# An RWKV-5 block followed by top-1 experts: rows stored in thirds, unpadded loads, weights and gathers asked for at other moments

## The chip, the cores and the metric

The kernel runs on one core of a Trainium2 chip. The core has a matrix engine (TensorE, PE in the profile, with PEld for its weight loads), VectorE (DVE), ScalarE (ACT), GpSimd (POOL), and SyncE (SP), which here does nothing but issue transfers. Sixteen DMA engines move data between device memory (HBM) and on-chip memory (SBUF); each engine's program issues its transfers in program order and waits on semaphores in that order too. The metric is the device time of one execution in microseconds (us), the median of several runs.

## The reference, cut to what matters

First comes an RWKV-5 recurrence over 4 batches, 8 heads, 768 steps and head size 48. Its result, 3072 rows of 384 numbers, goes through a switch layer: each row is sent to one of 8 experts (384 to 1024 to 384) by the largest gate logit, and scaled by its softmax weight.

```python
# attention: r, k, v (4, 8, 768, 48), w, u (8, 48)
state = np.zeros((B, H, D, D))
for t in range(S):
    kt, vt, rt = k[:, :, t], v[:, :, t], r[:, :, t]
    cur = np.einsum('bhd,bhe->bhde', u[None] * kt, vt)
    y[:, :, t] = np.einsum('bhd,bhde->bhe', rt, state + cur)
    state = w[None, :, :, None] * state + np.einsum('bhd,bhe->bhde', kt, vt)
x = y.transpose(0, 2, 1, 3).reshape(3072, 384)
# experts: w_gate (384, 8), w1 (8, 384, 1024), w2 (8, 1024, 384)
logits = x @ w_gate
expert_idx = np.argmax(logits, axis=1)
probs = softmax(logits)            # written out in the original
gate_w = probs[np.arange(N), expert_idx]
for e in range(E):
    mask = expert_idx == e
    out[mask] = gate_w[mask, None] * (np.maximum(x[mask] @ w1[e], 0.0) @ w2[e])
```

## The kernel before

The attention is worked off in 32 *units*: batch, half of the sequence (three chunks of 128 steps) and pair of heads, so that eight units make a batch and four a half. One turn of the loop over `u` loads unit u + 4, scales unit u + 2, forms the products of unit u + 1 and puts out unit u. Beside that, a half that is done goes through the gate (`u_gate`), and the rows of a done batch, with their gate weight as a 385th number, are stored to `x_hbm`, from where the expert part gathers them by index. The expert weights `w2` of all experts have one large tile; while the attention runs, the part for experts 4 to 7 serves as its ring of buffers.

```python
NW = E // 2                                    # 4 experts' w2 are loaded in the attention
ring = w2_all[:, NW:, :]                       # (flattened) the rest of w2's tile
rks = cut(4, 2 * HC * C)                       # r and k of a unit, 128 x 768 floats, 4 buffers
toks = cut(5, 4 * HC * D)                      # v and k by token, 128 x 576 floats, 5 buffers
...
xb_ring = cut(1, G * W)[0]...                  # rows of one batch, 6 x 385 floats per partition

def u_load(u):
    b, hf, hp = unit(u)
    nc.sync.dma_start(rks[u % 4], rk[b, hf, hp])      # heads at partitions 0-47 and 64-111, zeros between
    nc.sync.dma_start(toks[u % 5], tok[b, hf, hp])

def store_rows(b, xb, g0, g1):
    nc.sync.dma_start(x_hbm[b * S:(b + 1) * S, :]...[:, g0:g1], xb[:, g0:g1])

def weight():                                  # a step of choose(b, xb, lg)
    ...
    nc.vector.reciprocal(xb[:, :, DM], se)
    store_rows(b, xb, 0, HC)                   # first half of the batch's rows
return [shift, first, weight, lambda: store_rows(b, xb, HC, G)]
```

Scaling (lines 472 to 481) is what first needs a unit's loads:

```python
def u_scale(u, eng=nc.gpsimd):
    nc.gpsimd.tensor_tensor(x["RK"], x["r"], x["k"], op=ALU.mult)               # 472
    eng.tensor_tensor(x["K"], x["k"], bc(W2[:, hp, None, :], ...), op=ALU.mult) # 473
    nc.vector.tensor_tensor(x["R"], x["r"], bc(W1[:, hp, None, :], ...), op=ALU.mult)  # 474
def u_scale_g(u):
    nc.gpsimd.tensor_tensor(x["Kg"][:, 0:ns, :], x["kt"][:, 0:ns, :], ...)      # 481
```

The loop over units. `todo` holds the steps of the routing by turn: for batch b, with g = 8 (b + 1) + 2, `shift` in turn g, `first`, `weight` and the first store in g + 1, the second store in g + 2.

```python
for u in range(NU):
    if u + 4 < NU:
        u_load(u + 4)
    if HP <= u < HP + 4 * NW:
        w2_load((u - HP) // 4, u % 4, 4)       # a quarter of one expert's w2, 384 KB
    elif HP + 4 * NW <= u < HP + 4 * NW + NEARLY * FQ:
        tiles[(u - HP - 4 * NW) // FQ].load_w1(wp, u % FQ)
    if u + 2 < NU:
        u_scale(u + 2)
        u_scale_g(u + 2)
    if u + 1 < NU:
        if u:
            u_scores(u + 1)                    # products: lines 493, 503
        u_state(u + 1)
        u_mask(u + 1)
    u_out(u)
    ...
    for step in todo[u]:
        step()
```

Then comes the step to the experts. A *tile* is 128 rows of one expert: `load_x` gathers its rows (GpSimd, indirect), `turn` transposes them, `hidden` is the first product with ReLU (line 981), `result` the second (line 990) with the scaling by the gate weight, `store` scatters the rows to the output. Tiles t0 and t1 are known from the first two batches; their rows and w1 are loaded in the attention. All others need the last batch's routing (`ranks`, `bases`, `order`, `slots`, `owners`, `index`).

```python
weight()
rest()                                         # stores of the last batch's rows
w2_load(NW)
w2_load(NW + 1)                                # 1536 KB each
...
t2.load_w1(wp)
t0.result(mo)
t1.hidden(mo, 0)
R.index(rt, "rw")
t2.load_x(mo)
t3.load_x(mo)
t0.store()
for e in range(NW + 2, E):
    w2_load(e)
t1.hidden(mo, 1)
t3.load_w1(wp)
t1.result(mo)
t1.store()
t2.turn(mo, "g")
late = late_rows(R, NSURE - NEARLY, ...)       # 8 gathers: rows of tiles that run only if there are many
run_tiles(tiles[2:], wp, mo, Segments(R, 0))

def run_tiles(tiles, wp, mo, seg):
    for j, t in enumerate(tiles):
        if j + 2 < len(tiles):
            tiles[j + 2].load_x(mo)
        ...
        t.hidden(mo, 0)
        ...
        t.hidden(mo, 1)
        ...
        if j + 2 < len(tiles):
            tiles[j + 2].load_w1(wp)
        ...
        if j + 1 < len(tiles):
            tiles[j + 1].turn(mo, "g")
        t.result(mo)
        t.store()
```

`late_rows` makes up to 8 tiles whose rows are gathered in any case and which are computed only behind a test of a count; with these inputs none of them runs. Line numbers in the texts below are those of this kernel where it is the one spoken of.

Of the kernel before, what the change touches and what calls it, by code (L numbers as in the profile page):

```python
# [1 line left out]

# [20 lines left out]
HP = H // 2  # L23
# [18 lines left out]
NW = E // 2  # L42
# [9 lines left out]
def rwkv5_then_switch(ctx, tc, r, k, v, rk, tok, wu_in, wl, wg, wgh, w1, w2, out):  # L52
# [35 lines left out]
    xb_ring = cut(1, G * W)[0].rearrange("p (g d) -> p g d", g=G)  # L88

# [4 lines left out]
    def u_load(u):  # L94
        b, hf, hp = unit(u)
        nc.sync.dma_start(rks[u % 4], rk[b, hf, hp])
        nc.sync.dma_start(toks[u % 5], tok[b, hf, hp])
# [75 lines left out]
    def choose(b, xb, lg):  # L173
# [27 lines left out]
        return [shift, first, weight, lambda: store_rows(b, xb, HC, G)]  # L201

    def general():
# [166 lines left out]
        def gate(b, xb):  # L370
# [13 lines left out]
            for step in choose(b, xb, lg):  # L384
                step()

# [13 lines left out]
    def fast():  # L400
# [35 lines left out]
        def tables(hp):  # L436
            scaled(W2, Wr, hp, w_64)
            scaled(W1, Wp, hp, w_64)
# [131 lines left out]
        xbs = [xb_ring, la.tile([128, G, W], FP32, name="xb")]  # L570
# [50 lines left out]
        with tc.manual_schedule():  # L621
            tables(0)
# [52 lines left out]
            shift, first, weight, rest = chosen[B - 1]  # L675
# [4 lines left out]
            rest()  # L680
            w2_load(NW)
            w2_load(NW + 1)
# [243 lines left out]
    class Tile:  # L926
# [58 lines left out]
        def result(self, mo):  # L985
            p = self.R.ps.tile([128, DM], FP32, name="yp", tag="y", bufs=2)
            e = slice(self.j, self.j + 1) if self.early else ds(self.expert(ENG.PE), 1)
            for f in range(FT):
                rhs = w2_all[:, e, f * DM:(f + 1) * DM]
                nc.tensor.matmul(p, lhsT=self.hT[:, f, :], rhs=rhs, start=f == 0, stop=f == FT - 1)  # L990
# [73 lines left out]
    def run_tiles(tiles, wp, mo, seg):  # L1064


        for j, t in enumerate(tiles):
# [30 lines left out]
    def late_rows(R, first, rows):  # L1098


        late = [Tile(R, j, late=True) for j in range(first, NTILE)]
        late += [Segments(R, j, late=True) for j in range(1, E // NS)]
        for t, xs in zip(late, rows, strict=True):
            t.load_x(xs)
        return late
# [25 lines left out]
    def after_general():  # L1131
# [15 lines left out]
        with tc.manual_schedule():  # L1147
# [5 lines left out]
            late = late_rows(R, NSURE, [xl[:, i] for i in range(NTILE - NSURE + E // NS - 1)])  # L1153
            run_tiles(tiles, mo, mo, Segments(R, 0))
# [70 lines left out]
```

## Time and profile before

| | |
|---|---|
| device time, median of 3 runs | 442.06 us (441.38 to 442.60) |
| span of the profiled execution | 440.0 us |
| TensorE busy | 415.4 us (94%) |
| VectorE, ScalarE, GpSimd busy | 149.5, 127.5, 155.6 us |
| mean granted TensorE clock | 0.973 |
| moved by DMA | 101.7 MB, mean 231 GB/s |

The profile is one execution on the chip. A busy time is the sum of an engine's instructions. *The chain of waits* follows the execution back from its last instruction: at each step to what released it, or to the instruction before it on its engine; printed in order of time, its columns are the start, the duration, and what it was. *The timeline* lists instructions with start, duration, engine, line, operation, tiles and count; brackets hold the idle time in front and what ended it. SPq and POOLq are the issuing queues of SyncE and GpSimd: the duration there is that of the issue, not of the transfer. *The windows* give busy time of each engine in a stretch of time, the granted clock of TensorE, the share of time that the DMA engines were busy, and GB/s. The attention ends near 139 us (the first transposes of t0 stand at 139.07 us), t1's result at 164.7 us, the last matmul at 429.4 us.

### The profile page before, as it was taken

The numbers are of one execution on the slowest core, as the hardware profiler recorded it, in microseconds if no ns is written. First come the engines' busy times: TensorE is split into PE (matmuls) and PEld (weight loads), VectorE is DVE, ScalarE is ACT, GpSimd is POOL, SyncE is SP. The second block draws the span as 40 slices with busy tenths as digits, with TensorE's granted clock in tenths as the row PEclk, the third lists the DMA queues.
The fourth block names the chain that finished last, engine by engine and source line by source line (L and its number), as shares of the span: only waits on it lengthen the run. The fifth ranks groups of instructions, "written<-read, shape, count | busy, mean of one in ns | idle before, by whom it ended". The sixth has DMA issues, their size and how long they took to land.

```text
span 440.0 us, 10264 instructions
## 1 busy us (share of the span) xinstructions
PE 415.4 (94%) x4079; PEld 343.6 (78%) x4079; DVE 149.5 (34%) x407; ACT 127.5 (29%) x394; POOL 155.6 (35%) x189
## 2 busy tenths in 40 slices
PE   8899998997999997979999999999999999999990
PEld 8799997997999877758887878777878778787770
DVE  6576796896897840101111111010111111010100
ACT  3777775774765220101111111111110101111110
POOL 7997746945962027302111111111111101111100
PEclk9999999999899996989999999999999999999997
DMA  7488959959942899885886656665858585554100
GB/s 267 149 250 283 302 161 344 387 166 340 384 151 70 259 361 387 167 350 188 329 317 183 257 201 242 216 267 189 302 181 313 184 305 180 178 181 148 63 21 25
DMA packets 28704, 101.73 MB, mean 231 GB/s; under 512 B 4134, under 2 KB 7228, under 8 KB 25316
## 3 DMA queue, kind: packets, MB, share of 16 engines
q1 hardware_dynamic: 24642, 89.69, 57.2%
q0 software_dynamic: 3712, 11.23, 8.9%
q8 instruction: 37, 0.61, 0.6%
q14 instruction: 23, 0.19, 0.1%
q10 hardware_dynamic: 290, 0.02, 0.0%
HBM read 91.47 MB, written 9.65 MB: 230 GB/s over the span
## 4 chain that ended last, share of the span: by engine, by line
PE 81%; DMA 7%; POOL 3%; issue 3%; DVE 2%; ACT 1%; POOLq 0%; SPq 0%
PE hp L981 27%; PE yp L990 26%; PE P L503 5%; PE yp L564 4%; DMA w_all<-in_r_k_units_dram 4%; PE P L493 4%; DMA xs<-x_hbm,idx 3%; PE yp L560 3%; PE rp L593 3%; PE Gp L539 2%; PE xTp L968 2%; PE warm L110 2%; PE hg L1036 1%; PE yg L1056 1%; POOL xb L962 1%
## 5 line engine op out<-in xcount | busy, mean ns | idle before, releaser
L981 PEld LDWEIGHTS hp<-xT,w1s 128*128 128x128 f32 x1152 | 135.7, 195 | 11.2 <-issue 4.1
L981 PE MATMUL hp<-xT,w1s 128*128 128x128 f32 x1152 | 138.0, 279 | 0.6 <-DVE xT L970 0.6
L990 PE MATMUL yp<-w_all,hT 128*128 (+1 forms) x384 | 129.6, 491 | 0.6 <-ACT hT L983 0.6
L990 PEld LDWEIGHTS yp<-w_all,hT 128*128 128x128 f32 x384 | 71.8, 192 | 46.3 <-ACT hT L983 1.2
L983 ACT ACTIVATE hT<-hp 128x512 f32<-128x512 f32 x48 | 28.7, 597 | 238.0 <-PE hp L981 216.3
L995 POOL DMA_INDIRECT out_dram<-yo,idx x22 | 22.4, 1019 | 204.0 <-DVE yo L992 194.5
L514 ACT ACTIVATE A<-ident,dv 128x128 f32<-128x128 f32 x192 | 59.6, 389 | 0.2 <-ACT dv L511 0.2
L992 DVE TENSOR_SCALAR yo<-yp,xs 128x384 f32<-128x384 f32 x22 | 13.6, 618 | 106.2 <-PE yp L990 106.2
L970 DVE COPY xT<-xTp 128x384 f32<-128x384 f32 x23 | 12.8, 556 | 104.6 <-PE xTp L968 93.3
L472 POOL TENSOR_TENSOR w_all<-w_all 128x384 f32<-128x384 f32 x31 | 34.3, 1108 | 26.9 <-DMA w_all<-in_r_k_units_dram 13.0
L564 PE MATMUL yp<-A,w_all 128*64 128x128 f32 x384 | 41.5, 283 | 0.1
L525 DVE COPY_PREDICATED A<-mask,P 128x384 f32<-128x384 int32 x64 | 33.8, 583 | 8.0 <-ACT A L514 7.4
L560 PE MATMUL yp<-w_all,St 128*64 128x128 f32 x320 | 34.5, 282 | 0.2 <-ACT dv L511 0.2
L473 POOL TENSOR_TENSOR w_all<-w_all,W 128x384 f32<-128x384 f32 x31 | 33.6, 1085 | 0.0
L962 POOL DMA_INDIRECT xs<-x_hbm,idx x22 | 21.5, 976 | 31.6 <-PE hp L981 25.5
L503 PE MATMUL P<-w_all 48*128 48x128 f32 x384 | 30.2, 291 | 0.4
L493 PE MATMUL P<-wu,w_all 48*128 48x1 f32 x384 | 26.5, 249 | 4.0 <-POOL w_all L472 4.0
L493 PEld LDWEIGHTS P<-wu,w_all 48*128 48x128 f32 x384 | 24.0, 187 | 8.0 <-POOL w_all L472 4.5
L564 PEld LDWEIGHTS yp<-A,w_all 128*64 128x64 f32 x384 | 28.3, 142 | 0.9 <-DVE A L525 0.5
L474 DVE TENSOR_TENSOR w_all<-w_all,W 128x384 f32<-128x384 f32 x32 | 25.6, 804 | 6.9 <-DMA w_all<-in_r_k_units_dram 5.6
L481 POOL TENSOR_TENSOR w_all<-w_all,Wg 128x288 f32<-128x288 f32 (+1 forms) x32 | 24.9, 779 | 1.4 <-ACT dv L511 1.1
L503 PEld LDWEIGHTS P<-w_all 48*128 48x128 f32 x384 | 24.7, 191 | 0.8 <-POOL w_all L473 0.4
(164 smaller groups left out, 299.5 us busy)
## 6 DMA issues: line engine op xcount, KB each, us to landing
w1s<-in_moe_w_dram SPq DMA_DIRECT2D x22, 1536.0 KB
w_all<-in_r_k_units_dram SPq DMA_DIRECT2D x32, 384.0 KB
wq<-in_moe_w_dram SPq DMA_DIRECT2D x32, 384.0 KB
w_all<-in_v_k_units_dram SPq DMA_DIRECT2D x32, 288.0 KB
w_all<-in_moe_w_dram SPq DMA_DIRECT2D x16, 384.0 KB
w_all<-in_moe_w_dram SPq DMA_DIRECT2D x4, 1536.0 KB
w1s<-in_moe_w_dram SPq DMA_DIRECT2D x8, 384.0 KB
x_hbm<-w_all SPq DMA_DIRECT2D x4, 577.5 KB
```

Source lines behind the costliest of these rows:

```text
L472: nc.gpsimd.tensor_tensor(x["RK"], x["r"], x["k"], op=ALU.mult)
L473: eng.tensor_tensor(x["K"], x["k"], bc(W2[:, hp, None, :], [128, HC, C]), op=ALU.mult)
L493: nc.tensor.matmul(P[hi][:, o:o + 1], lhsT=x["RK"][q, c, :], rhs=wu[q, 1, hp:hp + 1], start=True, stop=True, skip_group_check=True)
L503: nc.tensor.matmul(P[hi][:, c * C:(c + 1) * C], lhsT=x["K"][q, c, :], rhs=x["R"][q, c, :], start=True, stop=True, skip_group_check=True)
L514: nc.scalar.activation(A[:, hi, c, :], ident, func=ACT.Copy, scale=dv[:, hi, c:c + 1])
L525: nc.vector.copy_predicated(A[:, hi], bc(mask[:, None, :].bitcast(I32), [128, HC, C]), P[hi][:, 0:HC * C].rearrange("p (c t) -> p c t", t=C))
L560: nc.tensor.matmul(yp[q, c, :], lhsT=old[:, hi, :], rhs=x["R"][:, c, :], start=True, stop=False, skip_group_check=True)
L564: nc.tensor.matmul(yp[q, c, :], lhsT=vh(x, c, hi, 64), rhs=x["A"][:, hi, c, :], start=old is None, stop=True, skip_group_check=True)
L962: nc.gpsimd.indirect_dma_start(out=self.xs, out_offset=None, in_=x_hbm[:, :], in_offset=off)
L981: nc.tensor.matmul(p[:, f, :], lhsT=self.w1[:, q, d, o:o + 128], rhs=self.xT[:, d, :], start=d == 0, stop=d == DT - 1)
L983: nc.scalar.activation(self.hT[:, 4 * fb:4 * fb + 4, :], p, func=ACT.Relu)
L990: nc.tensor.matmul(p, lhsT=self.hT[:, f, :], rhs=rhs, start=f == 0, stop=f == FT - 1)
```

## The change

Six things change. The rows of a batch go to memory in three parts of two chunks, one per turn in turns g + 1 to g + 3, and these turns carry no expert weights. Units from the fifth on load only the 48 rows of r and k that each head has, in two transfers; the padding stays zero from the first four. The rows of one batch move out of the ring, which then fits into three experts' place, so five experts' w2 are loaded in the attention instead of four, their pieces spread over the turns that store nothing, six of them ahead of the loop. The last three experts' w2 are asked for right behind the last batch's rows, where it was two there and two later. The transposes of t2 stand before the last two products of t1's result. And the eight late gathers are issued one per tile, from the seventh tile of the main loop on, where they stood together ahead of it. The purpose is to keep transfers that the next work waits for from queueing behind others. What is computed does not change.

```diff
-NW = E // 2
+NW = 5
-    xb_ring = cut(1, G * W)[0].rearrange("p (g d) -> p g d", g=G)
     def u_load(u):
         b, hf, hp = unit(u)
-        nc.sync.dma_start(rks[u % 4], rk[b, hf, hp])
+        if u < 4:
+            nc.sync.dma_start(rks[u % 4], rk[b, hf, hp])
+        else:
+            for hi in range(2):
+                q = slice(64 * hi, 64 * hi + D)
+                nc.sync.dma_start(rks[u % 4][q], rk[b, hf, hp, q])
         nc.sync.dma_start(toks[u % 5], tok[b, hf, hp])
 ...
             nc.vector.reciprocal(xb[:, :, DM], se)
-            store_rows(b, xb, 0, HC)
 ...
-        return [shift, first, weight, lambda: store_rows(b, xb, HC, G)]
+        return [shift, first, weight, lambda i, n: store_rows(b, xb, i * G // n, (i + 1) * G // n)]
 ...
-        xbs = [xb_ring, la.tile([128, G, W], FP32, name="xb")]
+        xbs = [ca.tile([128, G, W], FP32, name="xb0"), la.tile([128, G, W], FP32, name="xb1")]
 ...
+        stores = set()
         for b in range(B - 1):
             g = 2 * HP * (b + 1) + 2
-            for i in range(4):
-                todo[g + min(i, 1) + i // 3].append(lambda b=b, i=i: chosen[b][i]())
+            for i in range(3):
+                todo[g + min(i, 1)].append(lambda b=b, i=i: chosen[b][i]())
+            for i in range(3):
+                todo[g + 1 + i].append(lambda b=b, i=i: chosen[b][3](i, 3))
+                stores.add(g + 1 + i)
 ...
+        pieces = [lambda e=e, i=i: w2_load(e, i, 4) for e in range(NW) for i in range(4)]
+        n = 4 * (NW - 1)
+        pieces[n:n] = [lambda j=j, i=i: tiles[j].load_w1(wp, i) for j in range(NEARLY) for i in range(FQ)]
+        turns = [u for u in range(1, NU) if u not in stores]
+        ahead = len(pieces) - len(turns)
+        piece = dict(zip(turns, pieces[ahead:], strict=True))
         with tc.manual_schedule():
+            for load in pieces[:ahead]:
+                load()
 ...
-                if HP <= u < HP + 4 * NW:
-                    w2_load((u - HP) // 4, u % 4, 4)
-                elif HP + 4 * NW <= u < HP + 4 * NW + NEARLY * FQ:
-                    tiles[(u - HP - 4 * NW) // FQ].load_w1(wp, u % FQ)
+                if u in piece:
+                    piece[u]()
 ...
-            rest()
-            w2_load(NW)
-            w2_load(NW + 1)
+            rows(0, 2)
+            rows(1, 2)
+            for e in range(NW, E):
+                w2_load(e)
 ...
-            for e in range(NW + 2, E):
-                w2_load(e)
             t1.hidden(mo, 1)
             t3.load_w1(wp)
-            t1.result(mo)
+            t1.result(mo, lambda: t2.turn(mo, "g"))
             t1.store()
-            t2.turn(mo, "g")
-            late = late_rows(R, NSURE - NEARLY, [xbs[1][:, i] for i in range(G)] + [t0.xs, t1.xs])
-            run_tiles(tiles[2:], wp, mo, Segments(R, 0))
+            late = late_tiles_of(R, NSURE - NEARLY)
+            run_tiles(tiles[2:], wp, mo, Segments(R, 0), zip(late, [xbs[1][:, i] for i in range(G)] + [t0.xs, t1.xs],
+                                                             strict=True))
 ...
             for f in range(FT):
+                if within and f == FT - 2:
+                    within()
 ...
             t.result(mo)
             t.store()
+            if j >= 6:
+                for x, xs in islice(late, 1):
+                    x.load_x(xs)
```

(Cut: the same edits in the path for decays out of the usual range, which does not run with these inputs.)

More of the change, by code (lines that the diff above doesn't have):

```diff
@@ L1 @@
 from contextlib import ExitStack
+from itertools import islice
 import concourse.bass as bass
@@ L383, in gate @@
             nc.vector.tensor_copy(lg, lgp)
-            for step in choose(b, xb, lg):
+            *steps, rows = choose(b, xb, lg)
+            for step in steps:
                 step()
+            rows(0, 1)
         step = 0
@@ L674, in fast @@
             mo = em.enter_context(tc.tile_pool(name="mo", bufs=2))
-            shift, first, weight, rest = chosen[B - 1]
+            shift, first, weight, rows = chosen[B - 1]
             shift()
@@ L983, in hidden, with result @@
             nc.scalar.activation(self.hT[:, 4 * fb:4 * fb + 4, :], p, func=ACT.Relu)
-        def result(self, mo):
+        def result(self, mo, within=None):
             p = self.R.ps.tile([128, DM], FP32, name="yp", tag="y", bufs=2)
@@ L1062, in result, with run_tiles @@
             nc.vector.tensor_scalar_mul(self.y, self.p, self.xs[:, DM:W])
-    def run_tiles(tiles, wp, mo, seg):
+    def run_tiles(tiles, wp, mo, seg, late):
         for j, t in enumerate(tiles):
@@ L1096, in run_tiles, with late_tiles_of @@
                 seg.store()
[L1098 to L1105, printed above, removed]
+    def late_tiles_of(R, first):
+        return [Tile(R, j, late=True) for j in range(first, NTILE)] + \
+            [Segments(R, j, late=True) for j in range(1, E // NS)]
     def late_tiles(R, tiles):
@@ L1152, in after_general @@
             xl = rt.tile([128, NTILE - NSURE + E // NS - 1, W], FP32, name="xl")
-            late = late_rows(R, NSURE, [xl[:, i] for i in range(NTILE - NSURE + E // NS - 1)])
-            run_tiles(tiles, mo, mo, Segments(R, 0))
+            late = late_tiles_of(R, NSURE)
+            run_tiles(tiles, mo, mo, Segments(R, 0), zip(late, [xl[:, i] for i in range(len(late))], strict=True))
         em.close()
```

## The prediction

> **What bounds the kernel now.** I read the chain of waits first, because it says which engine's work sets the end.
>
> ```profile
> PE 81%; DMA 7%; POOL 3%; issue 3%; DVE 2%; ACT 1%; POOLq 0%; SPq 0%
> ```
>
> TensorE is the bound, and no part of the change removes a matmul. What can be won is TensorE's waiting, so I read the same chain in order of time and looked for long pieces that are not PE.
>
> ```profile
> 63.76 8.66 DMA w_all<-in_r_k_units_dram
> 72.58 0.57 POOL w_all L472
> ...
> 74.87 1.44 PE P L503 x12
> ...
> 97.24 9.06 DMA w_all<-in_r_k_units_dram
> ...
> 176.99 14.00 DMA xs<-x_hbm,idx
> 191.12 0.81 PE xTp L968 x3
> 191.93 6.60 PE yp L990 x16
> ```
>
> There are three: two loads of r and k that come late (units 17 and 25 of 32), and one gather of rows for the expert tiles. Third, busy time by stage. The columns after the stretch are its length, busy PE, PEld, DVE, ACT and POOL, granted clock, DMA share and GB/s.
>
> ```profile
> 72.00:76.00 4.00, 2.01 (x26) 1.88 (x24) 2.62 (x7) 0.77 (x3) 3.21 (x3) 0.89 1.03 405
> 76.00:80.00 4.00, 4.00 (x60) 3.65 (x59) 2.51 (x6) 2.83 (x10) 3.53 (x4) 0.68 1.04 400
> 164.00:168.00 4.00, 1.37 (x6) 0.39 (x4) 0.73 (x2) 0.00 (x0) 2.00 (x2) 0.91 1.05 414
> 168.00:172.00 4.00, 3.50 (x16) 3.50 (x17) 0.45 (x1) 0.00 (x0) 2.89 (x4) 0.50 0.96 390
> ```
>
> Each gap is paid twice: PE stands still, then runs at half clock for some microseconds. DMA is full in all four rows. Why the loads come late shows in SyncE's own timeline:
>
> ```profile
> 53.39 0.41 SPq L603 DMA_DIRECT2D w_all<-in_moe_w_dram  x1
> 60.71 0.39 SPq L171 DMA_DIRECT2D x_hbm<-w_all  x1
> ...
> 63.28 0.39 SPq L171 DMA_DIRECT2D x_hbm<-w_all  x1
> 63.76 0.44 SPq L96 DMA_DIRECT2D w_all<-in_r_k_units_dram  x1
> ```
>
> SyncE issues in order. It stands at the first store of a batch's rows for 6.9 us, until the gate weights exist, and then pours out two stores of 577.5 KB, with 672 KB of unit and 384 KB of expert weights for each turn between them. Last, the step from attention to the expert tiles:
>
> ```profile
> 159.33 5.33 PE L990 MATMUL yp<-w_all,hT 128*128 128x384 f32 x16
> 167.13 0.72 PE L968 MATMUL xTp<-ident,xs 128*128 128x128 f32 x3 [2.48 <-DMA xs<-x_hbm,idx]
> 168.50 8.30 PE L981 MATMUL hp<-xT,w1s 128*128 128x128 f32 x48 [0.65 <-DVE xT L970]
> 191.12 0.81 PE L968 MATMUL xTp<-ident,xs 128*128 128x128 f32 x3 [2.57 <-DMA xs<-x_hbm,idx]
> ```
>
> From 198.4 to 429.4 us PE is busy 4.00 of every 4 us; nothing is to be won there.
>
> [...] the load issued at 63.76 behind a store lands 8.66 us later. [...] issued from 159.49 to 160.48, the gather released PE at 167.1, so 6.6 us. I use 6.6. [...] Here gaps of 1.9 and 2.5 us were enough (0.50 from 168 to 173 us). [...] the multiplication of line 474 takes 0.55 us in the median and up to 3.05.
>
> **The change, part by part.**
>
> *Attention turns.* The cost of the two late loads comes from the starts of each unit's products (line 503) in PE's timeline. Units 5 to 13 take 29.2 us, units 13 to 21 take 33.5, units 21 to 29 take 34.5. In the undisturbed eight, the step into a second half (unit 9) is 3.27 us and the step after it 3.76. The same two steps take 5.47 and 5.37 us at units 17 and 18, so 3.8 us too much, and 5.79 and 5.38 at units 25 and 26, so 4.1 us too much. Together 7.9 us. (What is left over in those eights is the ranking matmuls, about 0.5 us a batch, and they stay.)
>
> Is this removed? SyncE still stands for the same 6.9 us, since the first third also waits for the weights. But behind it each of three turns now carries a third of the rows (385 KB) and an unpadded unit (48 of 64 rows of r and k: 288 KB, with v 576 KB) and no expert weights. Before, 2.98 MB moved from 61 to 72 us. Two stores are 1.18 MB; the rest at the 400 GB/s of the next row takes 4.5 us, which leaves 6.5 us, or about 180 KB/us, for the stores. After: two thirds at that pace 4.3 us, unit 16 and r, k of unit 17 (864 KB) 2.2 us. So unit 17's r and k land at about 61 + 6.5 + 1.5 = 69 us, an estimate, instead of 72.4; they are wanted at about 70.5 (PE would start that unit near 72, and line 472 takes 1.0). One to two microseconds of margin: I count both stalls as gone. The fourteen calm turns lose nothing: 576 + 384 KB in 3.76 us is 255 KB/us. The six weight pieces sent at the start (2.36 MB, 6 us) fall where DMA stood at 34% and 13% (12 to 20 us). One issue more per turn is 0.4 us of SyncE's 3.8.
>
> What takes something back is VectorE. Around the second stall it is busy 19.6 of 24 us (104 to 128); with the turns 4 us shorter that is 19.6 of 20. [...] I take back 1 us. Attention: -6.9 us.
>
> *First expert tile (t2).* Before, SyncE asked for experts 4 and 5 behind the last rows, for t2's first weights at 157.6, then for experts 6 and 7. Now expert 4 comes earlier and 5, 6 and 7 go right behind the rows. Bytes from 145.4 on: 1.18 + 4.72 MB. Before, 4.3 MB were through at 157.6; the remaining 1.57 MB take 3.8 us at 415 GB/s, so to 161.4; then t2's 1.57 MB, to 165.2; with its share for two gathers and completion, about 167. The gather of t2's rows is issued at the same moment against the same full DMA, so it should again land near 167. Two arrivals near 167 while PE is free at 163 to 165: **the first stall stays**. The transposes now stand before the last two products of t1's result (4 of the 16 records of 0.323 us): PE waits from 163.4 instead of 164.7, then has 1.3 us of work that covers the copy of 0.65. With half clock on it, even or 0.5 us worse. I take +0.5.
>
> *Second expert tile (t3).* The gather of 176.99 came behind eight late gathers, 1.3 us of issue each; they move into later tiles, so it is issued at 166.9 behind t1's store alone, and DMA is empty of bulk near 170. A calm tile takes 10.85 us (332.87 to 343.72 in the chain). Here, from 183.03 to 198.37, it took 15.34. Gain 4.5 us.
>
> *Later tiles.* Eight more gathers and their issue, one per tile, on a GpSimd that is busy 2 of 11 us. Nothing.
>
> Sum: 442.1 - 6.9 + 0.5 - 4.5 = 431.2 us.
>
> **The rivals.** *A: the first gather is freed too.* If the 6.6 us came from the three large loads queued at 158 and not from a full DMA as such, rows and weights might be there by 164. t2 then also runs at full clock: it lost 3.8 us of waiting and 14.53 - 10.85 = 3.7 us behind it, so up to 7 us more, about 424. For it: fewer bytes are left at 160 us (3.1 MB with t3's weights, where it was 5). Against: 3 MB is still 7 us of full DMA. I give it 0.25. *B: VectorE becomes the bound of the attention turns.* Then 3 to 4 us of the 7.9 stay, about 434. For it: 98% of the shortened stretch. Against: before the stall it idled 2.7 us waiting for the same load, and TensorE does not need a unit's mask until about 3 us after it. 0.2. *C: t2's weights come clearly later than the rows*, since they stand behind three experts instead of two: each microsecond beyond 167 costs one, with up to 3, about 434. 0.2. *D: late gathers among the tiles* hold back a tile's rows or weights. From 181 to 188 DMA moved only about 100 GB/s while gathers ran, so they are slow company; but rows are asked for nearly two tiles (20 us) ahead. 0.05.
>
> **Range and chances.** The middle is 431.2, with 0.25 x 7 us from A and smaller costs from B and C against it, so 430.0. Low end: A whole, 423.5. High end: B or C beside the rest, 435. Faster by 2% needs 433.2 or less; that fails only if attention gives 4 us or less, or if t2 loses 3: faster 0.80, same 0.19, slower 0.01.
>
> **What would show it.** In the changed profile the chain should hold no r, k load of 8 us; the steps into units 17, 18, 25 and 26 should be below 4.2 us; t2's transposes should still wait for rows or weights near 159 us (167 less 7 to 8) with half clock behind; t3 should take 10.9 us from hidden to hidden. The prediction is wrong if those steps stay above 5 us (the stores' issue, not their size, is the cause), if VectorE closes the gaps in PE, or if new waits stand among the later tiles.

## The result, and the profile after

The changed kernel takes 429.27 us (median; 426.78 to 430.15) where the kernel before took 442.33 us on the same chip: a ratio of 0.969, with a 95% interval of 0.963 to 0.975. The profiled execution has a span of 428.4 us, with TensorE busy for 408.6 us (95%). These lines of its page show the chain of waits by engine, and two groups: busy time and mean duration, then the idle time just before them and what ended most of it.

```profile
PE 88%; DMA 4%; DVE 1%; POOL 1%; issue 1%; ACT 0%; SPq 0%; POOLq 0%; DVEq 0%; ACTq 0%
...
L509 PE MATMUL P<-w_all 48*128 48x128 f32 x384 | 29.6, 286 | 1.5 <-DVE w_all L480 1.3
...
L499 PE MATMUL P<-wu,w_all 48*128 48x1 f32 x384 | 26.9, 249 | 1.3 <-POOL w_all L478 0.9
```

Line 509 is what was line 503, line 499 was 493, line 478 was 472. The load of r and k, twice in the chain of before with some 9 us each, does not end any idle time of TensorE now: what is left in front of the products is 1.3 us of VectorE, one wait ahead of unit 0 (9.34 us), and 0.9 us of GpSimd, one wait ahead of unit 29:

```profile
119.24 0.83 PE L499 MATMUL P<-wu,w_all 48*128 48x1 f32 x12 [0.90 <-POOL w_all L478]
```

SyncE's timeline at the first batch shows the thirds, one per turn, and that SyncE still stands in front of the first of them.

```profile
54.14 0.37 SPq L102 DMA_DIRECT2D w_all<-in_v_k_units_dram  x1
61.14 0.40 SPq L176 DMA_DIRECT2D x_hbm<-xb  x1
...
63.18 0.40 SPq L176 DMA_DIRECT2D x_hbm<-xb  x1
63.67 1.22 SPq L101 DMA_DIRECT2D w_all<-in_r_k_units_dram  x2
```

The loads of 63.67 are those of unit 17. GpSimd's timeline shows when they are there (the bracket is the idle time and what ended it):

```profile
71.20 1.22 POOL L478 TENSOR_TENSOR w_all<-w_all 128x384 f32<-128x384 f32 x1 [1.04 <-DMA w_all<-in_r_k_units_dram]
```

So they are there by 71.2 us, 1.4 us earlier than the 72.58 of before, and it is enough: the multiplication ends at 72.42, and TensorE comes to unit 17 at 72.91 without a wait. The step to the experts in TensorE's timeline:

```profile
153.33 4.04 PE L1009 MATMUL yp<-w_all,hT 128*128 128x384 f32 x12
160.71 0.88 PE L985 MATMUL xTp<-ident,xs 128*128 128x128 f32 x3 [3.35 <-DMA xs<-x_hbm,idx]
161.38 2.77 PE L1009 MATMUL yp<-w_all,hT 128*128 128x384 f32 x4
163.94 6.70 PE L998 MATMUL hp<-xT,w1s 128*128 128x128 f32 x48
...
175.97 5.52 PE L998 MATMUL hp<-xT,w1s 128*128 128x128 f32 x48
```

The first expert wait is still there (3.35 us, rows of t2), with half clock behind it; the second, at 191 us before, is gone. The windows (length, busy PE, PEld, DVE, ACT, POOL, granted clock, DMA share, GB/s) show the stretch around the second attention stall of before, now with VectorE and DMA nearly full and TensorE busy at full clock, and at the first expert tile a full DMA up to about 163 us and the clock at half behind the wait:

```profile
98.00:118.00 20.00, 19.71 (x365) 18.15 (x361) 18.44 (x49) 14.83 (x55) 14.78 (x17) 1.00 1.05 279
156.00:160.00 4.00, 1.37 (x5) 0.48 (x3) 0.00 (x0) 0.00 (x0) 1.02 (x1) 0.95 1.00 421
160.00:164.00 4.00, 3.29 (x8) 2.11 (x9) 0.56 (x1) 0.00 (x0) 0.00 (x0) 0.50 0.88 360
164.00:168.00 4.00, 4.00 (x27) 4.00 (x26) 0.62 (x1) 0.00 (x0) 1.99 (x2) 0.70 0.18 62
```

Where the time came from, read from the starts of the same instructions in both traces (us):

| stretch of TensorE's timeline | before | after | change |
|---|---|---|---|
| start to unit 0's products | 8.61 | 9.34 | +0.73 |
| unit 0 to unit 31 (attention) | 125.36 | 118.64 | -6.72 |
| unit 31 to t1's result | 25.36 | 25.35 | 0 |
| t1's result to t3's first hidden | 23.70 | 22.64 | -1.06 |
| t3's to t4's first hidden | 15.34 | 10.84 | -4.50 |
| t4's first hidden to the end | 241.63 | 241.59 | 0 |
| sum = difference of the spans | | | -11.6 |

Every microsecond is placed, but the first row's 0.73 has no account. Seven more traces with the changed attention (below) give 117.43 to 118.73 us for the second row, so such a stretch scatters over 1.3 us from trace to trace.

### The profile page after: what moved, and what is told of

It is laid out like the page before. It is cut to its first block, busy times and chain, and to the rows that moved or that the text cites. A ratio compares the mean times of both kernels' runs of the same rounds, so it can differ in the third digit from the quotient of the medians.

```text
span 428.4 us, 10349 instructions
## 1 busy us (share of the span) xinstructions
PE 408.6 (95%) x4079; PEld 338.2 (79%) x4079; DVE 146.6 (34%) x407; ACT 127.6 (30%) x394; POOL 152.5 (36%) x189
## 4 chain that ended last, share of the span: by engine, by line
PE 88%; DMA 4%; DVE 1%; POOL 1%; issue 1%; ACT 0%; SPq 0%; POOLq 0%; DVEq 0%; ACTq 0%
PE hp L998 28%; PE yp L1009 27%; PE P L509 6%; PE P L499 6%; PE yp L570 5%; PE rp L599 4%; PE yp L566 4%; PE Gp L545 3%; DMA w_all<-in_moe_w_dram 3%; PE xTp L985 2%; DMA xs<-x_hbm,idx 2%; PE hg L1055 1%; PE yg L1075 1%; PE warm L456 1%; POOL w_all L478 0%
## 5 line engine op out<-in xcount | busy, mean ns | idle before, releaser
L998 PE MATMUL hp<-xT,w1s 128*128 128x128 f32 x1152 | 136.4, 277 | 0.0
L570 PE MATMUL yp<-A,w_all 128*64 128x128 f32 x384 | 39.2, 274 | 0.1
L566 PE MATMUL yp<-w_all,St 128*64 128x128 f32 x320 | 32.4, 274 | 0.0
L479 POOL TENSOR_TENSOR w_all<-w_all,W 128x384 f32<-128x384 f32 x31 | 32.0, 1033 | 0.0
L570 PEld LDWEIGHTS yp<-A,w_all 128*64 128x64 f32 x384 | 25.6, 137 | 0.8 <-DVE A L531 0.5
L487 POOL TENSOR_TENSOR w_all<-w_all,Wg 128x288 f32<-128x288 f32 (+1 forms) x32 | 24.0, 751 | 4.1 <-ACT dv L517 2.0
L480 DVE TENSOR_TENSOR w_all<-w_all,W 128x384 f32<-128x384 f32 x32 | 23.3, 732 | 1.4 <-DMA w_all<-in_r_k_units_dram 1.3
```

Of the source, the lines that this page charges most:

```text
L479: eng.tensor_tensor(x["K"], x["k"], bc(W2[:, hp, None, :], [128, HC, C]), op=ALU.mult)
L566: nc.tensor.matmul(yp[q, c, :], lhsT=old[:, hi, :], rhs=x["R"][:, c, :], start=True, stop=False, skip_group_check=True)
L570: nc.tensor.matmul(yp[q, c, :], lhsT=vh(x, c, hi, 64), rhs=x["A"][:, hi, c, :], start=old is None, stop=True, skip_group_check=True)
L998: nc.tensor.matmul(p[:, f, :], lhsT=self.w1[:, q, d, o:o + 128], rhs=self.xT[:, d, :], start=d == 0, stop=d == DT - 1)
```

## The experiments

Absolute times differ from chip to chip (in the four sets of runs the kernel before took 442.33, 438.84, 437.44 and 438.78 us), so kernels are compared by their ratio to before or, more sharply, by the stretches of their traces. The kernels with padded loads, weights in store turns, and late gathers together or spread shared one chip; halves, all three undone, t3's weights behind the gather and two experts later a second; the rest a third.

### One measure of the attention undone at a time

Padded loads again:

```diff
-        if u < 4:
-            nc.sync.dma_start(rks[u % 4], rk[b, hf, hp])
-        else:
-            for hi in range(2): ...            # 48 rows of each head, 144 KB each
+        nc.sync.dma_start(rks[u % 4], rk[b, hf, hp])
```

> The changed kernel, but units from the fifth on load all 128 rows of r and k again, padding included, in one transfer of 384 KB instead of two of 144 KB. My theory in the prediction (fewer bytes buy the margin behind the stores): the loads behind the stores land about 1 us later, so the steps into units 17 and 25 go from 3.27 us to 4 to 5, and the time rises by 1 to 3 us (430 to 432). The rival (from the profile after: from 20 to 60 us SyncE's queue keeps the DMA engines busy 94.7% of the time for 10.15 MB, where before it was 77.9% for 10.25 MB, so a transfer to 48 rows is the dearer one): the queue's share falls back to about 78%, the steps stay below 4 us, and the time is the same within 1 us (428 to 430).

Weight pieces in the turns that store:

```diff
-        turns = [u for u in range(1, NU) if u not in stores]
+        turns = list(range(HP, HP + len(pieces) - 6))
```

> The changed kernel, but the 22 weight pieces of the loop stand in turns 4 to 25, as before, so that six of the nine turns that store a third also carry a piece of 384 KB. If keeping the weights out of the store turns is what frees the loads: the steps into units 17 and 18 and into 25 and 26 grow by 1 to 4 us in each of the two groups, and the time rises by 2 to 7 us (431 to 436). If thirds instead of halves are enough: no step above 4.5 us and the same time within 1 us.

Rows in two halves:

```diff
-            for i in range(3):
-                todo[g + 1 + i].append(lambda b=b, i=i: chosen[b][3](i, 3))
-                stores.add(g + 1 + i)
+            for i in range(2):
+                todo[g + 1 + i].append(lambda b=b, i=i: chosen[b][3](i, 2))
+            for i in range(3):
+                stores.add(g + 1 + i)
```

> The changed kernel with the rows of a batch stored in two halves again (turns g + 1 and g + 2) instead of three thirds; the turn g + 3 keeps its freedom from weights, and all else stays. Theory: what freed the loads is fewer bytes queued in front of unit 17's and 25's r and k; a half in front of them instead of a third is 193 KB more per turn, about 0.5 to 1 us at 180 to 400 KB/us, inside the margin of 1 to 2 us: units 13 to 21 and 21 to 29 stay within 1 us of the changed kernel's 30.30 and 31.68 us. Rival: the thirds are what counts, since a store moves slowly (180 KB/us); then the steps at 17 and 18 go back above 5 us each and each group of eight takes 33 us or more, 3 to 5 us more in all.

And the three edits together:

> The changed kernel with all three attention measures undone together: padded loads of r and k (384 KB), weight pieces in the turns that store, rows in two halves. What stays is five experts' weights in the attention, six pieces ahead of the loop, and all of the expert part. Singly, padding cost 1.1 us from unit 0 to unit 31 and weights in the store turns 3.5 us. Theory: the measures are one, namely bytes queued ahead of the load that the next turn wants; undone together they bring back both stalls whole, 6 to 8 us more than the changed kernel's 118.64 us (about 125 to 126). Rival: one measure alone does it; then the sum is near the largest single one, 3.5 to 4 us more, about 122.

Measured (steps between the starts of consecutive units' products; the undisturbed pair is 3.27 and 3.76 us):

| kernel | steps into 17, 18 | into 25, 26 | unit 0 to 31 | ratio to before, interval |
|---|---|---|---|---|
| before | 5.47, 5.37 | 5.79, 5.38 | 125.36 | |
| changed | 3.27, 3.76 | 3.27, 3.77 | 118.64 | 0.969 (0.963 to 0.975) |
| changed, again | 3.27, 3.76 | 3.27, 3.77 | 118.17 | 0.976 (0.971 to 0.981) |
| padded loads | 3.89, 3.87 | 3.27, 3.81 | 119.78 | 0.977 (0.968 to 0.986) |
| weights in store turns | 4.14, 4.50 | 3.97, 4.17 | 122.22 | 0.981 (0.973 to 0.989) |
| halves | 3.27, 3.76 | 3.83, 3.90 | 120.11 | 0.983 (0.977 to 0.989) |
| all three | 4.63, 3.89 | 5.08, 5.50 | 122.46 | 0.992 (0.989 to 0.994) |

By the ratios alone the three single edits can't be told from the changed kernel, which is 0.969 on one chip and 0.976 on another; what follows rests on one trace of each. No single measure brings a stall of before back. With padded loads the step into unit 17 is 3.89 us and the one into 25 unchanged, so below 4 as the rival said, not the 4 to 5 of the theory, and the DMA share is as the rival had it (below); of the 1.1 us more from unit 0 to unit 31, 0.7 us are lost there (steps into 17 and 18). Beside it, TensorE waits 1.12 us for VectorE ahead of unit 27, and not the 0.90 us for GpSimd ahead of unit 29. Weights in the store turns cost 1.6 us at units 17 and 18 and 1.1 at 25 and 26, the low end of what was expected. That edit costs 3.6 us in all, but not all of it is the queue: 2.2 us is one wait at unit 31, where GpSimd had two early gathers of rows to issue right ahead of the multiplication that TensorE wanted; without it this edit is worth no more than the other two. TensorE's and GpSimd's timelines of that kernel:

```profile
130.31 0.83 PE L499 MATMUL P<-wu,w_all 48*128 48x1 f32 x12 [2.24 <-POOL w_all L478]
```

```profile
126.25 1.25 POOL L975 DMA_INDIRECT xsA<-x_hbm,idxA  x1 [0.30 <-POOL xsA L974]
...
128.22 1.00 POOL L975 DMA_INDIRECT xsA<-x_hbm,idxA  x1 [0.28 <-POOL xsA L974]
129.25 1.00 POOL L478 TENSOR_TENSOR w_all<-w_all 128x384 f32<-128x384 f32 x1
```

The halves cost nothing at units 17 and 18 and 0.7 us at 25 and 26. The kernel with two experts' weights later (below) has thirds and 3.98 and 3.88 us at units 25 and 26, so it is not shown that thirds are worth anything over halves. (Another 1.75 us at unit 20 of that kernel, 5.51 instead of 3.76, has an idle time of 1.41 us that the profile gives no cause for; a step of 4.50 us stands at the same place in one kernel with thirds. It stays open, and it is the larger part of this kernel's 1.5 us.) With all three undone, the second stall is back nearly whole, 10.58 us for the two steps against 11.17 before. The first is not. TensorE's timeline of the kernel with all three undone shows why the two differ:

```profile
73.58 0.83 PE L494 MATMUL P<-wu,w_all 48*128 48x1 f32 x12 [1.02 <-POOL w_all L473]
...
105.29 0.83 PE L494 MATMUL P<-wu,w_all 48*128 48x1 f32 x12 [1.47 <-POOL w_all L473]
```

A wait of 1.02 us was followed by full clock (groups of four products at 0.39 us, as undisturbed; step 3.89), one of 1.47 us by half clock (granted 0.50 from 109 to 111 us, groups of four at 0.60 to 0.64 us; step 5.50), and before, 1.86 us by half clock too (0.50 from 76 to 78 us; step 5.37). Both theory (6 to 8 us back) and rival (3.5 to 4) put a number on this: 3.8 us came back in this trace, the rival's number (the traced run, 431.56 us, is among the faster of its kernel, whose median is 433.72, so that 3.8 is at the low end). But the rival's reason does not hold, since no measure alone brings a stall back and the second stall is nearly whole; the number is about what one whole stall makes. The 2.9 us that did not come back are 2.3 us at the first stall and 0.6 at the second; what else in the change holds them was not separated.

The four kernels order the same way at unit 17 by both measures. GpSimd starts its multiplication at 71.14 us with padded loads, at 71.69 with weights in the turns, at 72.25 with all three undone, at 72.58 before; the step into unit 17 is 3.89, 4.14, 4.63, 5.47 us. (Unit 16 began between 69.40 and 69.92 us in these four. In the first trace of the changed kernel it began at 70.33, so that 71.20 was still in time; in its second at 69.57, with the multiplication at 70.22.)

Padded loads had a surprise: the unpadded ones are the dearer for DMA. The calm stretch from 20 to 60 us in the windows of the changed kernel, and then of the one with padded loads:

```profile
20.00:60.00 40.00, 40.00 (x746) 36.90 (x744) 28.21 (x76) 30.43 (x112) 31.13 (x41) 1.00 0.96 257
```

```profile
20.00:60.00 40.00, 40.00 (x743) 36.95 (x743) 30.48 (x75) 30.82 (x114) 34.12 (x43) 1.00 0.81 279
```

The last two numbers are the DMA share and GB/s: with unpadded loads the engines are busy 0.96 of the time for 257 GB/s, with padded ones 0.81 for 279 (before: 0.79 for 259). The issues of the same stretch (KB each, median us to landing), changed and then padded:

```profile
w_all<-in_r_k_units_dram SPq DMA_DIRECT2D x20, 144.0 KB, 7.4
```

```profile
w_all<-in_r_k_units_dram SPq DMA_DIRECT2D x9, 384.0 KB, 5.3
```

Fewer bytes, and they land 2 us later. Why is not shown: the unpadded load writes 48 partitions at a time where the padded one writes 128, and it is two transfers of 144 KB where that is one of 384 KB, and no run separates the two. In this kernel TensorE is busy all 40 us either way, so nothing was lost.

### The late gathers

All eight together again in the changed kernel, and alone spread in the kernel before:

```diff
-            run_tiles(tiles[2:], wp, mo, Segments(R, 0), zip(late, [...], strict=True))
+            for x, xs in zip(late, [...], strict=True):
+                x.load_x(xs)
+            run_tiles(tiles[2:], wp, mo, Segments(R, 0), iter(()))
```

> The changed kernel, but the eight late gathers are issued together ahead of the main loop, as before. If these gathers hold up the rows of t4: they are issued from about 166.4 to 176.8 us, t4's gather behind them lands near 184, three microseconds after its transposes are due at 181.3, and with the half clock behind it the third tile takes 14 to 15.4 us instead of 10.84; the time rises by 3 to 4.5 us (432 to 434). The rival, that they were slow only because the weights of two experts and of t3 filled the DMA beside them: after 164 us the DMA is nearly empty now, nine gathers at 1.3 us of issue end near 180, and the third tile stays at 10.8 to 11.2 us, the time at 428 to 430.

```diff
-            late = late_rows(R, NSURE - NEARLY, [...])          # kernel before
-            run_tiles(tiles[2:], wp, mo, Segments(R, 0))
+            late = late_tiles_of(R, NSURE - NEARLY)
+            run_tiles(tiles[2:], wp, mo, Segments(R, 0), zip(late, [...], strict=True))
```

> The kernel before, with one part of the change alone: the eight late gathers one per tile. If they alone made t4's rows late: the third tile goes from 15.34 us to about 10.9, the attention and t2 stay as before, and the time falls by 4 to 5 us (437 to 438). The rival (the weights of experts 6 and 7, asked for late, were the cause): t4's gather, asked for at 166.9 us, meets a DMA that is full until 176, still lands before it is needed at 188, but t2's end and the weights cost the same; if the rival holds, less than 2 us are won (440 to 442).

Measured: together, ratio 0.990 (0.988 to 0.992), and from t3 to t4 14.88 us; spread in the kernel before, 0.992 (0.990 to 0.994), and 10.84 us from t3 to t4 where before had 15.34, with the attention as before (125.01 us). TensorE's timeline with the gathers together:

```profile
184.21 0.52 PE L986 MATMUL xTp<-ident,xs 128*128 128x128 f32 x3 [3.10 <-DMA xs<-x_hbm,idx]
```

As the theory had it: putting them together brings this wait back, spreading them takes it away. The 4.0 to 4.5 us belong to this edit alone and add to the rest. One thing differs from the expectation: the half clock that it counted on did not come in this trace. Behind the wait of 3.10 us t3's second product took 5.42 us and t4's first 5.52, against 5.33 and 5.52 in a calm tile; the wait alone, with slower pieces around it, makes the 14.88 us. And the edit is worth a little more than that, which the prediction did not see. With the gathers together, t2's second product waits for ScalarE:

```profile
172.44 2.85 PE L1010 MATMUL yp<-w_all,hT 128*128 x8 [1.65 <-ACT hT L1001]
```

Before, this wait was 0.63 us; with the gathers spread it is absent, in the kernel before with that edit alone too, where t1's result to t3's hidden falls from 23.70 to 23.13 us.

### The first expert tile: what the gather waits for

t3's first weights behind the rows of t2: a transfer of 4 bytes that reads a gathered row stands ahead of them in SyncE's queue.

```diff
             t1.hidden(mo, 1)
+            nc.sync.dma_start(mark_hbm, t2.xs[0:1, 0:1])
             t3.load_w1(wp)
```

> The changed kernel with one 4-byte transfer that reads t2's gathered rows put into SyncE's queue ahead of t3's first weights, so that these 1.5 MB are asked for only when t2's rows have landed. Theory: the gather of t2's rows takes 6 to 7 us because the DMA engines are full until 163.4 us, so with 1.5 MB (3.6 us) less in front DMA runs dry near 160 us, the rows land 1 to 2 us earlier and the wait ahead of t2's transposes falls from 3.35 us to 1.5 to 2.5. Rival: the gather has a latency of its own of 6 us whatever else moves; then the wait stays 3.0 to 3.6 us.

Two experts' weights later, as before:

```diff
-            for e in range(NW, E):
-                w2_load(e)                     # right behind the last rows
+            w2_load(NW)
...
             t0.store()
+            for e in range(NW + 1, E):
+                w2_load(e)
             t1.hidden(mo, 1)
```

> The changed kernel with only the sixth expert's second weights right behind the last rows, and the last two experts' asked for behind t0's store, as the kernel before asked for its last two. Theory: where the weights stand in the queue changes only which bytes go first, not how long DMA is full; t2's own weights come some 4 us earlier, its rows do not, so the wait ahead of t2's transposes stays at 3 to 4 us and the step from t1's result to t3 is the same within 0.7 us. Rival 1: t2's rows are faster (DMA is emptier when they are asked for): the wait falls below 2.5 us. Rival 2: the 3 MB behind the rows collide with the gather: the wait rises above 4 us and the gain of 1.06 us on t2 is lost.

Measured against the gather's issue: with t3's weights behind it the wait is 3.15 us, the latency 6.85 us (152.33 to 159.18), ratio 0.982 (0.977 to 0.987). With two experts later, 3.96 us and 7.66 us, ratio 0.985 (0.980 to 0.990), and from t1's result to t3's hidden 23.28 us, 0.6 more than the changed kernel's 22.64: within what the theory allowed, at its edge, and neither rival's number; the two traces of the changed kernel, 22.64 and 21.53, lie further apart than that. The wait of 3.15 us is the rival's number (3.0 to 3.6), not the theory's (1.5 to 2.5). The changed kernel has 3.35 and 7.06 (153.65 to 160.71). The windows of the first of these two:

```profile
156.00:158.00 2.00, 0.03 (x1) 0.00 (x0) 0.00 (x0) 0.00 (x0) 0.00 (x0) 1.00 0.93 381
158.00:160.00 2.00, 0.82 (x4) 0.85 (x5) 0.00 (x0) 0.00 (x0) 0.00 (x0) 0.72 0.37 142
```

DMA was nearly full to 158 us, 5.7 us behind the gather's issue: three experts' and t2's own weights were enough. So this run, which met the rival's number, does not settle whether a full DMA or something of the gather's own makes the wait; it only shows that t3's weights are not what holds the rows. The next two do.

Everything that t2 was thought not to need, behind the gather:

```diff
-            for e in range(NW, E):
-                w2_load(e)                     # right behind the last rows
...
             t1.hidden(mo, 1)
+            nc.sync.dma_start(mark_hbm, t2.xs[0:1, 0:1])
             t3.load_w1(wp)
+            for e in range(NW, E):
+                w2_load(e)
```

> The changed kernel with everything that t2 does not need put behind the gather of its rows: one 4-byte transfer that reads the gathered rows, then t3's first weights, then the second weights of experts 5, 6 and 7. Ahead of the gather only the stores of the last rows and t2's own first weights (1.5 MB) remain. Theory: the gather is slow because it shares full DMA engines from its issue on (6.8 to 7.9 us), and on an emptier DMA it takes 3.1 us, as the gathers behind 164 us in the changed kernel; here t2's weights run dry near 155.5 us, so the rows land 3 to 5 us after the issue, the wait ahead of the transposes falls below 1.5 us and no half clock follows: 3 to 4.5 us less than the changed kernel, if no later tile waits for weights. Rival: part of the 6.8 us belongs to these two gathers whatever DMA does (indices just written, rows just stored); then the wait stays above 2.5 us and nothing is gained.

The same without the 4-byte transfer, and the changed kernel again on that chip:

> As the kernel with all late weights behind the gather, but without the 4-byte transfer that waits for the rows: t2's and then t3's first weights and the three experts' second weights are asked for as soon as their buffers are free. It tells the order of the requests from the moment of their issue. Theory (full DMA makes the gather slow): t3's weights and 4.5 MB more come up right behind t2's, DMA stays full over the whole gather, and the wait stays at 3 to 4.5 us as in the kernel with two experts' weights later (3.96 us). Rival (only the bytes queued ahead of the gather count): fewer bytes are ahead of it than in the changed kernel, so the wait falls to 1.5 us or less.

> The changed kernel itself, unchanged, beside the other kernels of this call, so that they can be compared with it on one chip. Expected: 0.965 to 0.985 of the kernel before; unit 0 to unit 31 in 118 to 119.5 us; the wait ahead of t2's transposes 3.0 to 3.7 us, with half clock behind it; t3 to t4 10.85 us.

| kernel | gather of t2's rows, issue to TensorE's start | wait | ratio to before, interval |
|---|---|---|---|
| changed, again | 7.06 (152.85 to 159.91) | 3.33 | 0.976 (0.971 to 0.981) |
| all behind the gather | 5.18 (152.12 to 157.30) | 1.46 | 1.005 (1.002 to 1.008) |
| all behind t3's weights | 7.74 (153.10 to 160.84) | 4.03 | 1.000 (0.997 to 1.004) |

TensorE's timeline of the kernel with all behind the gather, and its windows:

```profile
157.30 0.52 PE L987 MATMUL xTp<-ident,xs 128*128 128x128 f32 x3 [1.46 <-DMA xs<-x_hbm,idx]
...
158.95 5.52 PE L1000 MATMUL hp<-xT,w1s 128*128 128x128 f32 x48
...
178.10 7.59 PE L1011 MATMUL yp<-w_all,hT 128*128 x16 [13.30 <-DMA w_all<-in_moe_w_dram]
```

```profile
144.00:148.00 4.00, 4.00 (x29) 3.34 (x28) 3.85 (x8) 1.04 (x1) 0.00 (x0) 1.00 0.00 0
```

The theory's half that was at stake came true: with fewer bytes around it the same gather took 1.9 us less, the wait fell to 1.46 us and no half clock followed (granted 1.00 up to 168 us; t2's hidden 5.52 us, not 6.2). That is at the upper edge of the 3 to 5 us expected: DMA ran dry only some 5 us behind the issue. Without the mark it took 7.74, though less stood ahead of it: bytes asked for and not yet moved when the gather was issued were 2.8 MB there and 3.5 MB in the changed kernel, an estimate from the issues and the windows. In that kernel DMA was busy 0.97 to 1.04 of each 2 us from 152 to 162 us; in the one with all behind the gather it was busy 0.28 of the us from 157 and 0.00 of the next. So in these runs it is the full DMA that makes the gather slow, and not only what stands ahead of it. Whether a part of the 5.18 us is the gather's own stays open. The other half of my expectation, "if no later tile waits", fell hard: t2's second product waits 13.3 us for the expert weights, and without the mark 5.34 us. The chain names the load that it waits for, the last of the three:

```profile
159.60 18.25 DMA w_all<-in_moe_w_dram
```

Which expert a tile from t2 on belongs to is known only at run time, so its product reads the weights at an index, and what is seen is that it waits for the last load into that tile (landed at 177.85 us, product at 178.10). So these 4.7 MB are wanted within t2, and DMA stood empty from 144 us (0.00 of the next 4 us, and of 2 more) while they waited. Asking for them right behind the rows, as the changed kernel does, is right, and it is also what fills DMA when the gather comes. A way out would be a sixth expert's weights in the attention; their place in `w2`'s tile serves as the ring of buffers there, and it was not tried.

### Where t2's transposes stand

```diff
-            t1.result(mo, lambda: t2.turn(mo, "g"))
+            t1.result(mo)
             t1.store()
+            t2.turn(mo, "g")
```

> The changed kernel with t2's transposes behind t1's result and store again, as before. Theory: their place matters little, since TensorE waits for the rows either way; standing behind, the four last products (1.3 us at full clock) run ahead of the wait, so the wait is 1.3 us shorter (about 2.0 to 2.5 us), but the copy of the transposed rows (0.65 us) is then waited for: from the start of t1's result to the start of t2's hidden the time is the same within 0.7 us (10.61 us in the changed kernel). Rival: the early place is worth the copy and the half-clock products, 1.3 us or more.

Ratio 0.973 (0.968 to 0.979), beside 0.976 (0.971 to 0.981) for the changed kernel on that chip: no difference. TensorE's timeline:

```profile
160.12 0.53 PE L986 MATMUL xTp<-ident,xs 128*128 128x128 f32 x3 [2.02 <-DMA xs<-x_hbm,idx]
161.30 8.48 PE L999 MATMUL hp<-xT,w1s 128*128 128x128 f32 x48 [0.65 <-DVE xT L988]
```

From t1's result (152.77) to t2's hidden it is 8.53 us, 1.5 to 2.1 less than the changed kernel's 9.98 and 10.61, so the expectation of 0.7 missed; but t2's hidden then takes 8.48 us, with 0.50 granted from 161 to 167 us, instead of 6.22 and 6.70. To t3's hidden it is 22.34 us, between the 21.53 and 22.64 of the changed kernel's two traces. The products go ahead of the wait or behind it, and the half clock is paid by whichever comes behind (the four products took 2.77 and 2.46 us in the changed kernel's traces, 1.46 in the kernel with all behind the gather). The edit is worth nothing here.

## Why the prediction was right, point by point

- **Sum and range.** Predicted 430.0 us, measured 429.27. That it is so close is partly luck: the 430.0 is the sum of 431.2 less a share for rival A, which did not happen, and t2, which was to lose 0.5 us and gained 1.06, filled the same place.
- **Attention, -6.9 us: measured -6.7 (-7.2 in the second trace).** Both stalls are gone, steps 17, 18, 25 and 26 are the undisturbed 3.27 and 3.76 us. But the way there was mis-sized. Unit 17's r and k, "about 69 us, an estimate", were there by 71.2 in this trace and by 69.8 to 70.6 in the seven others, so about 1 us late as a rule, 2.2 at most; and the margin of 1 to 2 us was 0.5 us in this trace (72.42 to 72.91) and 0.3 to 1.6 in the others. The padded kernel shows what lies behind it: with the same start of the multiplication, 71.14 us, and an earlier unit 16 its step already loses 0.6 us. The sum had only two thirds and 864 KB, about 1.7 MB, moving until then; from 61 to 71 us DMA moved 2.57 MB (share 0.92, 257 GB/s), so some 0.9 MB that the sum did not count moved ahead of r and k or beside them. And the 1.5 us in "61 + 6.5 + 1.5" has no working.
- **VectorE takes back 1 us.** The size was the author's estimate. About that was taken back, but not by VectorE. From 98 to 118 us it is busy 18.44 of 20 us (predicted 19.6), and TensorE's one wait for it, 1.3 us, stands ahead of unit 0; in the turns it waits 0.90 us for GpSimd, at unit 29, and 0.29 us with no cause that the profile names. Of the 7.9 us of stalls 6.7 were won, so 1.2 us came back: units 13 to 21 take 30.30 us and 21 to 29 31.68 us, 0.6 and 1.3 us above before less its stalls (33.51 - 3.8 and 34.49 - 4.1), and the two steps into units 30 and 31 are 0.7 us shorter than before. The size was right, the engine was not, and that is luck. Rival B did not happen in this kernel, but a wait of that kind is seen in the padded one (1.12 us for VectorE ahead of unit 27).
- **t2, +0.5 us: measured -1.06 (-2.2 in the second trace).** The step's core held: the wait is still there, for the rows, with half clock behind. Two sizes failed. The gather took 7.06 us where before's took 7.64 by the same measure (159.49 to 167.13), so 0.4 us less from t1's result to the transposes. And the four products behind the wait were counted as extra half-clock time; the half clock lasted 6.8 us before (from 167.31) and 6.8 us after (from 159.57, while TensorE still waited until 160.71), so that t2's hidden got back what the wait and the products took of it (8.30 to 6.70 us). The 0.63 us wait for ScalarE within t2's result went as well; that belongs to the late gathers, as the kernel with that edit alone shows.
- **t3, -4.5 us: measured -4.50,** from the late gathers alone, as both experiments on them show, and about half of what t2 gained is theirs too.
- **Later tiles, nothing:** 241.63 and 241.59 us. Rival D did not happen.
- **Rival A** (the first gather freed) did not happen, for the reason given against it, a full DMA (0.96 to 1.04 from 156 to 162 us); the kernel with all behind the gather shows that its mechanism exists (5.18 us where the changed kernel has 7.06), and that it can't be had by order alone, as t2's second product wants the same bytes. **Rival C** (t2's weights last) did not happen: t2's hidden starts behind the products without a wait.

## What to carry to other kernels

A load that comes late can cost twice (before, 2.48 us of waiting ahead of t2 and 2.8 more in its hidden, 8.30 us for 5.52), so shorten the queue ahead of the loads that the next step wants: move what is not urgent (here weights, 3.6 us in all, and late gathers, 4.0 to 4.5 us) to turns that have room, and expect that a few tenths of lateness can cost more than themselves, because a wait may or may not bring half clock (in the kernel with all three undone 1.02 us did not, step 3.89 us behind it; 1.47 us did, step 5.50). Before moving a load back, look at who waits for it behind the stall that you want to remove: the kernel with all weights behind the gather won 1.9 us at one tile and lost 13.3 us at its next product. And fewer bytes were not less DMA time here (0.96 of it busy for 257 GB/s unpadded, 0.81 for 279 padded): read share and landing, not KB.

## What the runs showed that was not expected

- Unpadded loads to 48 partitions kept DMA busier than padded ones to 128 (0.96 for 257 GB/s against 0.81 for 279) and landed 2.1 us later (7.4 against 5.3 us).
- Half clock does not follow from the length of the gap alone. After gaps of 1.47, 1.86 and 2.48 us it came (after the first of these 2.7 us behind the gap's end, when TensorE was long busy again), and after one of 3.33 us ahead of t2 (the changed kernel's second trace); after one of 3.38 us at the same place (the kernel with all three measures undone) the granted clock was 1.00 in each us from 161 to 179. Nor does it start at one distance from the gap: worked out from the granted clock of short windows, it starts in the kernel before at 75.15, 109.28, 167.31 and 191.20 us, which is 1.24, 1.49, 0.18 and 0.08 us behind the ends of the gaps, and in the changed kernel at 159.57 us, 1.14 us ahead of the end. What decides it is not shown. Where it came ahead of t2's hidden or within it, it lasted 3.4 us (3.42 in the changed kernel's second trace and with t3's weights behind the gather) or 6.8 us (before, with the transposes behind, and in the changed kernel's first trace). From t1's result to t3's hidden the changed kernel's two traces differ by 1.1 us (22.64 and 21.53), with half clock of 6.8 and 3.4 us.
- A gather of 128 rows took 6.9 to 7.7 us from its issue under a full DMA and 5.2 us where DMA ran dry 5 us after the issue; behind 164 us in the changed kernel, where DMA is busy 0.58 of the time, 20 gathers of rows took 3.3 us in the median. At t2 no packet of the gather's queue moves in the first 4.1 us behind its issue, while SyncE's queue moves 1.77 MB and its packets take 101.8% of the engines' time (DMA view of 153.6 to 157.7 us).
